# Routing steps inside an attention loop: a table laid out the other way round, built a unit later, and VectorE's routing steps put after its attention steps

## The chip, the cores and the metric

One core of a Trainium2 chip. The metric is the device time of one execution in microseconds, the median of several runs.

## The reference

A gated linear attention over 768 steps (4 batches, 8 heads of 40) gives 3072 rows of 320 numbers. Each row goes through a mixture of 8 experts (two of them for each row, chosen by noisy logits), each expert being a product 320 to 1024, a ReLU and a product 1024 to 320:

```python
C = f_stab * C + i_stab * einsum('bhd,bhe->bhde', v_t, k_t);  n = f_stab * n + i_stab * k_t
y_t = sigmoid(o_t) * (C @ q_t) / maximum(abs(n . q_t), 1)          # 768 steps, 32 (batch, head) pairs
logits = x @ w_gate + log1p(exp(x @ w_noise)) * noise
top2, top2_w = the two largest logits and their softmax
out[mask_e] += top2_w * (relu(x[mask_e] @ w1[e]) @ w2[e])          # for each expert e
```

## The kernel before

**Attention, units 0 to 23.** The sequence is cut into 12 chunks of 64 steps; a unit is one chunk of 16 (batch, head) pairs, so there are 24 units. The loop `while i < NU - LEAD` runs 22 of them, the last two are written out after it. The order of every engine is the order in which the program is written; nothing is rescheduled. In unit i TensorE (PE) does `c_part` (L385, state update), `o_part` (L394, output of the unit), the first `e_part` product (L334, gate exponents of unit i+2), `l_part` (L437, gate logits), at times the ranks `r_part` (L446 to L448) or a burst `b_part` (L457), the transposes `t_part` (L417), the second `e_part` product, and `s_part` (L354, L357, scores of unit i+2). ScalarE (ACT) copies the state (`c_part`, L388), takes the exponentials (L337), part of the sigmoid (`sig_part`, L343), and copies the transposes (L421) and logits (L515). VectorE (DVE) does `k_part` (kd, L365), the three steps of `f_part` (dn, dn, tm: L399, L401, L405) and `p_part` (p, L371), which the next unit's `o_part` needs. GpSimd (POOL) multiplies by the gate (L406) and issues part of the DMAs. The second `e_part` product writes the same PSUM bank as the first, so it waits for the first exponential.

**Routing, between the attention's steps.** Every four units make a group with a generator `g_part(g)`: softplus of the noise (na, co, ln: L540 to L559), top two (MAX, MAX_INDEX: L567, L570), counts `m` and prefix sums `base`, a request for ranks, and from the ranks two one-hot tables in fp16: `OB` (128 places, L652) and `OA` (56 blocks of 128 places of the experts' lists, L646, times a signed token number, L649). The burst of the group is eight matmuls with `OB[:, :, j]` as weights and `OA[:, :, j]` as the moving operand; their sum is added to the table `TBL`, from which token lists are decoded and rows gathered. `fill(upto, much)` takes steps of the waiting generators up to a sum of assumed prices: 0.2 at the unit's start, 0.15 between the steps of `f_part`, and what is left of 1.6 at the unit's end. A generator that yields `"long"` goes on only at the unit's end; one that yields `"wait"` stops for this call. ScalarE's part of the routing (Exp, +1, Ln: three instructions at L712, and Exp of d) is held in a list `acts` and issued by `act`: what stood in it at the unit's start behind the unit's first exponential, the rest at the unit's end. `next(pre1)` in the units of `W1AT` splits a piece of the first expert's weights into a high part (ScalarE, L142, L144) and a low part (POOL, L145).

**Experts.** After the last unit expert 0 begins with the tokens of the first 12 units: eight products `mm1` (f = 0 to 7, each eight matmuls at L1022 into one of three PSUM banks; ScalarE L1033 and VectorE L1036 read it), then second-layer sums in three passes (L1138). In between, `advance` does the remaining groups' routing: ranks and bursts come due at a set distance (`lag`) after they are asked for. After the burst of group 4, VectorE adds to the table (L464) and decodes, POOL gathers the rows of two more tiles (L794), and TensorE transposes them (L824) in the third pass.

Of the kernel before, what the change touches and what calls it, by code (L numbers as in the profile page):

```python
# [9 lines left out]
BF = mybir.dt.bfloat16  # L10
HF = mybir.dt.float16
# [3 lines left out]
OP = mybir.AluOpType  # L15
# [3 lines left out]
NE, F, DM = 8, 1024, 320  # L19
# [8 lines left out]
TC = BLK // 128  # L28
# [28 lines left out]
W1LD, W1AT, W2AT = (6, 9, 12, 15, 18), (11, 13, 17, 19, 20, 21), 21  # L57

C_ID, C_DIM, C_TRI, C_ONE, C_I8, C_TOK, C_N, C_SGN, C_VAC, C_COL, C_END = 0, 128, 192, 320, 448, 456, 480, 608, 656, 712, 768
# [6 lines left out]
def build(ctx, tc, qk, vk, og, fi, noise, wgn, w1, w2, cst, ce, out):  # L66
    nc = tc.nc
    V, A, P, T, SP = nc.vector, nc.scalar, nc.gpsimd, nc.tensor, nc.sync
# [10 lines left out]
    cs = keep.tile([128, C_END], F32, name="cs")  # L79
# [4 lines left out]
    cols = keep.tile([128, NE * TC, 8], HF, name="cols")  # L84
    sgn = keep.tile([128, 2 * NU], HF, name="sgn")
# [253 lines left out]
    def sig_part(u, ps_=(0, 1, 2)):  # L339

        g = SG[u % 4]
        for p in ps_:
            A.activation(g, g, (AF.Exp, AF.Ln, AF.Exp)[p], bias=float(p == 1), scale=(-1.0, 1.0, -1.0)[p])  # L343
# [64 lines left out]
    def keep_rows(u):  # L408
        (P if u < XV - 1 else SP).dma_start(XD[128 * u:128 * u + 128, 0:DM], XR[u])
# [119 lines left out]
    OAT = [rt.tile([128, NE * TC, 8], HF, name=f"oa{i}", bufs=1) for i in range(2)]  # L529

    def g_part(g):
# [14 lines left out]
        while acts:  # L546
            yield "wait"
        co = sm("co", [128, nb, NE])
# [33 lines left out]
        m = sm("m", [128, NE, nb + 1], BF)  # L582
        V.tensor_add(m[:, :, 1:].rearrange("p e u -> p u e"), oh4[:, :, 0], oh4[:, :, 1])
        if u0 == 0:

            V.tensor_scalar(m[:, :, 0], cs[:, C_I8:C_I8 + 8], 32.0, None, op0=OP.mult)
        else:
            V.tensor_copy(m[:, :, 0], acc[g - 1])
# [5 lines left out]
        asked = [m[:, :, 1:], base[:, :, 0:nb], base[:, :, nb], rk, False, unit[0] + lag[0]]  # L594
        want.append(asked)
        yield
        while acts:
            yield "wait"
        dd = sm("dd", [128, nb])
# [34 lines left out]
        n = 2 * nb  # L634
# [6 lines left out]
        while done[0] < u0 - 4:  # L641
            yield "wait"
# [3 lines left out]
        V.tensor_tensor(OA, cols, ah[:, None, :].to_broadcast([128, C, n]), op=OP.is_equal)  # L646
        yield 0.3
        yield "long"
        V.tensor_mul(OA, OA, sgn[:, None, 2 * u0:2 * u0 + n].to_broadcast([128, C, n]))  # L649
        yield 0.3  # L650
# [3 lines left out]
        bursts.append(([OB[:, :, j] for j in range(n)], [OA[:, :, j] for j in range(n)], unit[0] + lag[1]))  # L654
# [287 lines left out]
    sig_part(u + 1)  # L942
    keep_rows(u)
# [454 lines left out]
```

## Time and profile before

| what | us |
|---|---|
| median of 3 runs (517.52 to 518.98) | 517.7 |
| the profiled execution | 516.41 |
| its span, first to last instruction | 514.5 |
| TensorE busy in the span | 498.1 (97%) |
| VectorE, ScalarE, POOL busy | 332.2, 246.4, 231.2 |
| attention, as the units run | to about 127 |

The profile tells for each engine when each instruction ran and what it had waited for. A bracket such as `[0.42 <-DVE p L371]` behind a row is idle time of that engine just before it, and the instruction that ended it. Matmuls overlap and their ends are modelled, so a busy TensorE can hide short delays: the time from start to start tells more than the bracket. The granted clock is 0.997 of full speed over the span.

### The profile page before, as it was taken

Reading aid. Unit: us, or ns where it says so; the run is one execution under the profiler, and the core shown is the slowest. Engines: PE = TensorE matmul, PEld = TensorE weight load, DVE = VectorE, ACT = ScalarE, POOL = GpSimd, SP = SyncE. Lnnn points to the kernel's source line nnn. Section 1 sums busy time; section 2 is a strip of 40 time slices with the busy share of each in tenths; the row PEclk is TensorE's granted clock in tenths of the full one; section 3 lists DMA queues with packets and bytes.
Section 4 is the critical chain, followed back from the end, with each engine's and each line's share of the span. In section 5 each row is a group of like instructions: output and inputs, shape, how many; then the busy total and the mean of one; then the engine's idle time right before and its main releaser. Section 6 shows DMA issues by size and latency. Waiting matters only on the chain.

```text
span 514.5 us, 13117 instructions
## 1 busy us (share of the span) xinstructions
PE 498.1 (97%) x5042; PEld 471.6 (92%) x5043; DVE 332.2 (65%) x933; ACT 246.4 (48%) x568; POOL 231.2 (45%) x303
## 2 busy tenths in 40 slices
PE   8799999999999999999999999999999999999995
PEld 3588888888989998999999999999999999999994
DVE  7888889889695686754854584376538347555410
ACT  7689878889613354433541553153335405514300
POOL 9666674374034676156225604540562255142033
PEclk9999999999999999999999999999999999999998
DMA  6899787886848375196149406832951583282033
GB/s 168 234 277 250 220 240 192 231 229 204 314 134 261 70 96 184 46 245 145 41 99 270 104 16 160 209 89 52 268 101 49 129 234 89 56 177 26 2 35 47
DMA packets 51621, 77.06 MB, mean 150 GB/s; under 512 B 10825, under 2 KB 41936, under 8 KB 51520
## 3 DMA queue, kind: packets, MB, share of 16 engines
q1 hardware_dynamic: 38576, 50.16, 33.4%
q0 software_dynamic: 12976, 25.99, 24.8%
q8 instruction: 42, 0.69, 0.6%
q14 instruction: 27, 0.22, 0.1%
HBM read 52.27 MB, written 17.48 MB: 136 GB/s over the span
## 4 chain that ended last, share of the span: by engine, by line
PE 88%; DVE 3%; DMA 3%; POOL 2%; ACT 2%; issue 1%; SPq 0%; POOLq 0%; DVEq 0%
PE s L1022 25%; PE e L1022 12%; PE o L1054 5%; PE o L1053 5%; PE o L1052 5%; PE st L1054 5%; PE st L1052 5%; PE st L1053 5%; PE o L394 3%; PE s L357 3%; PE st L385 2%; PE e L334 2%; DMA vk<-vk_in 2%; PE xt L437 2%; PE xt L417 1%
## 5 line engine op out<-in xcount | busy, mean ns | idle before, releaser
L1075 POOL DMA_INDIRECT y_out<-y,tok x53 | 87.3, 1648 | 181.3 <-DVE y L1065 180.4
L1033 ACT ACTIVATE hx<-s 128x384 fp32r<-128x384 f32 (+5 forms) x91 | 44.4, 488 | 104.0 <-PE s L1022 66.7
L1022 PE MATMUL s<-xh,w1h 128*128 128x384 f32 (+5 forms) x273 | 76.4, 337 | 0.0
L1036 DVE SCALAR_TENSOR_TENSOR hx<-s,hx 128x384 fp32r<-128x384 f32 (+3 forms) x91 | 48.2, 529 | 36.5 <-ACT hx L1033 36.0
L794 POOL DMA_INDIRECT xg<-rows,tok x53 | 56.2, 1061 | 27.7 <-issue 12.8
L1022 PE MATMUL s<-xh,w1l 128*128 128x384 f32 (+5 forms) x273 | 62.4, 336 | 0.0
L1054 PE MATMUL o<-w2h,hx 128*128 128x320 f32 x184 | 56.8, 309 | 0.0
L1052 PE MATMUL o<-w2h,hx 128*128 128x320 f32 x184 | 56.8, 309 | 0.0
L1053 PE MATMUL o<-w2l,hx 128*128 128x320 f32 x184 | 56.7, 308 | 0.0
L1052 PE MATMUL st<-w2h,hx 128*128 128x320 f32 x176 | 54.4, 309 | 0.0
L1054 PE MATMUL st<-w2h,hx 128*128 128x320 f32 x176 | 54.4, 309 | 0.0
L1053 PE MATMUL st<-w2l,hx 128*128 128x320 f32 x176 | 54.2, 308 | 0.0
L1022 PEld LDWEIGHTS s<-xh,w1h 128*128 128x128 f32 x273 | 48.8, 188 | 1.8 <-ACT xh L826 0.3
L1022 PEld LDWEIGHTS s<-xh,w1l 128*128 128x128 f32 x273 | 47.8, 188 | 1.7 <-DVE xh L828 0.2
L1033 ACT ACTIVATE hx<-e 128x384 fp32r<-128x384 f32 (+5 forms) x45 | 22.1, 491 | 53.9 <-PE e L1022 36.7
L1022 PE MATMUL s<-xl,w1h 128*128 128x384 f32 (+5 forms) x182 | 46.3, 336 | 0.0
L1065 DVE TENSOR_SCALAR y<-o,gw 128x320 f32<-128x320 f32 x23 | 12.7, 551 | 47.2 <-PE o L1054 47.2
L1065 DVE TENSOR_SCALAR y<-st,gw 128x320 f32<-128x320 f32 x22 | 12.1, 551 | 43.5 <-PE st L1054 43.4
L1022 PE MATMUL e<-xh,w1h 128*128 128x384 f32 (+5 forms) x135 | 38.7, 341 | 0.0
L343 ACT ACTIVATE vk<-vk 128x320 f32<-128x320 f32 x72 | 33.8, 470 | 3.6 <-DMA vk<-og_in 2.7
L406 POOL TENSOR_TENSOR xr<-tm,vk 128x320 f32<-128x320 f32 x24 | 21.0, 875 | 30.9 <-ACT w L337 13.0
L1036 DVE SCALAR_TENSOR_TENSOR hx<-e,hx 128x384 fp32r<-128x384 f32 (+3 forms) x45 | 24.0, 534 | 16.4 <-ACT hx L1033 16.2
(243 smaller groups left out, 1252.4 us busy)
## 6 DMA issues: line engine op xcount, KB each, us to landing
raw<-w_in SPq DMA_DIRECT2D x6, 1280.0 KB
qk<-qk_in SPq DMA_DIRECT2D x24, 256.0 KB, 4.8
raw<-w_in SPq DMA_DIRECT2D x6, 1024.0 KB, 8.8
y_out<-zrow SPq DMA_DIRECT2D x15, 320.0 KB, 4.1
raw<-w_in SPq DMA_DIRECT2D x17, 256.0 KB, 9.7
vk<-vk_in POOLq DMA_DIRECT2D x24, 162.0 KB, 4.2
vk<-vk_in SPq DMA_DIRECT2D x24, 162.0 KB, 4.6
vk<-og_in SPq DMA_DIRECT2D x24, 160.0 KB, 4.2
```

The costliest lines, as they stand in the source:

```text
L343: A.activation(g, g, (AF.Exp, AF.Ln, AF.Exp)[p], bias=float(p == 1), scale=(-1.0, 1.0, -1.0)[p])
L357: T.matmul(SQ[u][:, p][half[p], h, :], q[r, 1, h, :], q[r, 0, h, :], start=True, stop=True)
L406: P.tensor_mul(XR[u], tm.rearrange("p h d -> p (h d)"), SG[u % 4])
L794: P.indirect_dma_start(out=XG[0:rows_of(t), t], out_offset=None, in_=XD[0:n], in_offset=bass.IndirectOffsetOnAxis(ap=token(e, t), axis=0), ...
L1022: T.matmul(ps[:, 0:n], l, r, start=i == 0, stop=i == len(ops) - 1)
L1033: A.activation(hi, x, AF.Relu)
L1036: V.scalar_tensor_tensor(lo, top[0], 0.0, top[1].bitcast(F32), op0=OP.max, op1=OP.subtract)
L1052: T.matmul(ps, HH[:, j, c], W2H[:, j], start=j == 0, stop=False)
L1053: T.matmul(ps, HH[:, j, c], W2L[:, j], start=False, stop=False)
L1054: T.matmul(ps, HLO[:, j, c], W2H[:, j], start=False, stop=j == 7)
L1065: V.tensor_scalar(y[0:n], ps[0:n], GW[e][0:n, t:t + 1], None, op0=OP.mult)
L1075: st = P.indirect_dma_start(out=out, out_offset=bass.IndirectOffsetOnAxis(ap=token(e, t), axis=0), in_=y[0:n], in_offset=None, compute_op= ...
```

## The change

- `OA` is now laid out `[128, 8, 56]`, so that each matmul's moving operand is 56 numbers in a row; before it was every eighth number of `[128, 56, 8]`. The one-hot comparison goes into a new tile `ohc` in the old layout, and the multiplication by the token number reads `ohc` with its last two axes turned.
- Both table steps and `OB` wait for the next unit (`unit[0] == begin`).
- Two new `"long"` marks, behind the waits for ScalarE: the steps from `co` on, and those from `dd` on, now go only at a unit's end, after `p`.
- The first column of `m` is written by POOL, ahead of `co`, and no longer by VectorE after the one-hots.
- Group 4's ranks (asked for in unit 19) come one unit later. `W1AT` becomes 11, 12, 16, 19, 20; the sixth piece is done in the written-out unit 22.

```diff
-W1LD, W1AT, W2AT = (6, 9, 12, 15, 18), (11, 13, 17, 19, 20, 21), 21
+W1LD, W1AT, W2AT = (6, 9, 12, 15, 18), (11, 12, 16, 19, 20), 21
-    OAT = [rt.tile([128, NE * TC, 8], HF, name=f"oa{i}", bufs=1) for i in range(2)]
+    OAT = [rt.tile([128, 8, NE * TC], HF, name=f"oa{i}", bufs=1) for i in range(2)]
...
         while acts:
             yield "wait"
+        yield "long"
+        m = sm("m", [128, NE, nb + 1], BF)
+        if u0 == 0:
+            P.tensor_scalar(m[:, :, 0], cs[:, C_I8:C_I8 + 8], 32.0, None, op0=OP.mult)
+        else:
+            P.tensor_copy(m[:, :, 0], acc[g - 1])
         co = sm("co", [128, nb, NE])
...
-            V.tensor_copy(m[:, :, 0], acc[g - 1])
...
-        asked = [..., rk, False, unit[0] + lag[0]]
+        asked = [..., rk, False, unit[0] + lag[0] + (unit[0] == 19)]
...
         while acts:
             yield "wait"
+        yield "long"
         dd = sm("dd", [128, nb])
...
-        while done[0] < u0 - 4:
+        begin = unit[0]
+        yield
+        while done[0] < u0 - 4 or unit[0] == begin:
             yield "wait"
...
-        V.tensor_tensor(OA, cols, ah[:, None, :].to_broadcast([128, C, n]), op=OP.is_equal)
+        OH = sm("ohc", [128, C, n], HF)
+        V.tensor_tensor(OH, cols, ah[:, None, :].to_broadcast([128, C, n]), op=OP.is_equal)
...
-        V.tensor_mul(OA, OA, sgn[:, None, 2 * u0:2 * u0 + n].to_broadcast([128, C, n]))
-        yield 0.3
+        V.tensor_mul(OA, OH.rearrange("p c j -> p j c"), sgn[:, 2 * u0:2 * u0 + n, None].to_broadcast([128, n, C]))
+        yield 0.5
...
-        bursts.append(([OB[:, :, j] for j in range(n)], [OA[:, :, j] for j in range(n)], unit[0] + lag[1]))
+        bursts.append(([OB[:, :, j] for j in range(n)], [OA[:, j] for j in range(n)], unit[0] + lag[1]))
...
     sig_part(u + 1)
+    next(pre1)
     keep_rows(u)
```

VectorE in unit 10 (dn, dn, tm, p are the attention's; co to nl and the MAX are group 1's routing; kd is the next unit's), before and after:

```order
L399 RECIPROCAL dn<-o 128x8
L549 SCALAR_TENSOR_TENSOR co_1379<-t_4_1320,ue_1319 128x32
L401 SCALAR_TENSOR_TENSOR dn<-dn 128x8
L551 RECIPROCAL na_1317<-t_4_1320 128x32
L405 SCALAR_TENSOR_TENSOR tm<-dn,o 128x320
L371 TENSOR_TENSOR p<-s,w 128x1024
L553 TENSOR_TENSOR co_1379<-co_1379,na_1317 128x32
```

```order
L399 RECIPROCAL dn<-o 128x8
L401 SCALAR_TENSOR_TENSOR dn<-dn 128x8
L405 SCALAR_TENSOR_TENSOR tm<-dn,o 128x320
L371 TENSOR_TENSOR p<-s,w 128x1024
L556 SCALAR_TENSOR_TENSOR co_1431<-t_4_1331,ue_1330 128x32
L558 RECIPROCAL na_1318<-t_4_1331 128x32
L560 TENSOR_TENSOR co_1431<-co_1431,na_1318 128x32
```

co and na, which need ScalarE's three routing instructions, moved from between dn and tm to behind p. ScalarE in unit 14 and at the start of unit 15 (w is an exponential, ue, t and ln are group 2's routing, share copies a burst's result, vk the state and the sigmoid), before and after:

```order
L337 ACTIVATE w<-e 128x512
L712 ACTIVATE ue_1743<-na_1741 128x32
L712 ACTIVATE t_4_1744<-ue_1743 128x32
L712 ACTIVATE ln_1745<-t_4_1744 128x32
L421 ACTIVATE xts<-xt 128x384
L515 ACTIVATE lg<-xt 128x16
L466 ACTIVATE share<-xt 128x56
L337 ACTIVATE w<-e 128x512
L343 ACTIVATE vk_114<-vk_114 128x320 x2
L388 ACTIVATE vk_111<-st 40x328 x2
```

```order
L337 ACTIVATE w<-e 128x512
L421 ACTIVATE xts<-xt 128x384
L515 ACTIVATE lg<-xt 128x16
L466 ACTIVATE share<-xt 128x56
L337 ACTIVATE w<-e 128x512
L717 ACTIVATE ue_1758<-na_1745 128x32
L717 ACTIVATE t_4_1759<-ue_1758 128x32
L717 ACTIVATE ln_1760<-t_4_1759 128x32
L343 ACTIVATE vk_114<-vk_114 128x320 x2
L388 ACTIVATE vk_111<-st 40x328 x2
```

The three moved from behind the unit's first exponential to behind its second, ahead of the next unit's state copy. VectorE in expert 0 around the last first-layer product, f = 7 (hx from bank e; rank to ob are group 4's, ln and nl group 5's), before and after:

```order
L632 TENSOR_SCALAR ai_2983<-rank 128x8
L1036 SCALAR_TENSOR_TENSOR hx<-s_2961,hx 128x384
L1114 TENSOR_TENSOR w2l<-raw_122,w2h 128x320
L637 SCALAR_TENSOR_TENSOR bi_2998<-ai_2983,rank 128x8
L640 CAST ah_3000<-ai_2983 128x8
L646 TENSOR_TENSOR oa_218<-cols,ah_3000 128x448
L649 TENSOR_TENSOR oa_218<-oa_218,sgn 128x448
L652 TENSOR_TENSOR ob_216<-spot,bi_2998 128x1024
L1036 SCALAR_TENSOR_TENSOR hx<-e,hx 128x384
L1114 TENSOR_TENSOR w2l<-raw_122,w2h 128x320
L559 TENSOR_TENSOR ln_2934<-ln_2934,nzt 128x32
```

```order
L634 TENSOR_SCALAR ai_2994<-rank 128x8
L1042 SCALAR_TENSOR_TENSOR hx<-e,hx 128x384
L1120 TENSOR_TENSOR w2l<-raw_122,w2h 128x320
L639 SCALAR_TENSOR_TENSOR bi_3003<-ai_2994,rank 128x8
L642 CAST ah_3005<-ai_2994 128x8
L651 TENSOR_TENSOR ohc_3009<-cols,ah_3005 128x448
L654 TENSOR_TENSOR oa_218<-ohc_3009,sgn 128x448
L657 TENSOR_TENSOR ob_216<-spot,bi_3003 128x1024
L556 SCALAR_TENSOR_TENSOR co_3021<-t_4_2964,ue_2963 128x32
L558 RECIPROCAL na_2942<-t_4_2964 128x32
```

The read of bank e for f = 7 now stands ahead of the table steps; group 5's steps from co on stand behind them. On TensorE the ranks of group 4 moved from behind f = 6 to behind f = 7, and its burst from the first pass of the sums to the second.

## Rows read from the trace of the kernel before

**Rows 1.** Busy time in the units' stretch: us, each engine's busy (instructions), clock.

```profile
26.00:123.30 97.30, 94.34 (x2244) 84.08 (x2240) 84.99 (x264) 83.08 (x216) 57.01 (x92) 1.00 0.87 233
```

**Rows 2.** Timeline of PE: start, us, instruction, count, [idle before <- what ended it].

```profile
74.88 0.18 PE L447 MATMUL xt<-base,ones 128*128 128x32 bf16 x1 [0.23 <-DVE base L591]
...
76.70 0.84 PE L385 MATMUL st<-vk,kd 104*40 104x41 f32 x32
77.96 1.13 PE L394 MATMUL o<-vk,p 104*64 104x41 f32 x32 [0.42 <-DVE p L371]
...
82.79 1.13 PE L394 MATMUL o<-vk,p 104*64 104x41 f32 x32 [0.22 <-DVE p L371]
...
87.37 0.81 PE L385 MATMUL st<-vk,kd 104*40 104x41 f32 x31
88.01 0.22 PE L394 MATMUL o<-vk,p 128*64 128x41 f32 x1
...
113.98 0.18 PE L446 MATMUL xt<-m,tri 128*128 128x32 bf16 x1 [0.41 <-DVE m L588]
...
120.16 0.50 PE L334 MATMUL e<-re,le 98*128 98x512 f32 x1 [0.48 <-ACT w L337]
```

**Rows 3.** The bursts and the ranks by line: duration ns min/median/max, first and last start.

```profile
L457 PEld LDWEIGHTS <-ob x48: 142/147/208, 65.0 to 158.9; 128*128 128x128 f16 x48
L447 PEld LDWEIGHTS <-ones x6: 95/95/101, 55.9 to 149.1; 128*128 128x128 bf16 x6
```

**Rows 4.** Timeline of the weight loads, the first burst.

```profile
65.03 0.90 PEld L457 LDWEIGHTS <-ob 128*128 128x128 f16 x8
```

**Rows 5.** Busy time of L712 in unit 14: us, ScalarE busy (instructions).

```profile
84.00:86.00 2.00, 0.69 (x3) 1.00 0.59 173
```

**Rows 6.** Timeline of ScalarE, units 10, 14 to 15, and 21.

```profile
67.09 0.62 ACT L337 ACTIVATE w<-e 128x512 f32<-128x512 f32 x1
...
87.19 0.99 ACT L343 ACTIVATE vk<-vk 128x320 f32<-128x320 f32 x2
88.25 0.89 ACT L388 ACTIVATE vk<-st 40x328 f32<-40x328 f32 x2
...
122.17 0.63 ACT L142 ACTIVATE w1h<-raw 64x512 fp32r<-64x512 f32 x1
```

**Rows 7.** Timeline of VectorE, units 10 and 11.

```profile
65.76 0.19 DVE L549 SCALAR_TENSOR_TENSOR co<-t,ue 128x32 f32<-128x32 f32 x1 [1.22 <-ACT t L712]
...
67.68 0.29 DVE L553 TENSOR_TENSOR co<-co,na 128x32 f32<-128x32 f32 x1
...
71.04 1.40 DVE L375 TENSOR_TENSOR p<-s,w 64x512 f32<-64x512 f32 x2
```

**Rows 8.** Timeline of POOL, a weight split in units 11 to 12.

```profile
72.92 1.27 POOL L145 TENSOR_TENSOR w1l<-raw,w1h 128x512 fp32r<-128x512 f32 x1 [0.80 <-DMA qk<-qk_in]
```

**Rows 9.** Timeline of VectorE in the same stretch, and the next kd.

```profile
73.04 1.26 DVE L583 TENSOR_TENSOR m<-oh 128x32 bf16<-128x32 f32 x1
...
74.75 0.80 DVE L365 TENSOR_TENSOR kd<-vk,w 128x640 f32<-128x640 f32 x1
```

**Rows 10.** The multiplication by the token number, by line: duration ns min/median/max.

```profile
L649 DVE TENSOR_TENSOR oa<-oa,sgn x6: 391/392/394, 59.8 to 152.9; 128x448 f16<-128x448 f16 x6
```

**Rows 11.** Timeline of PE in expert 0, the sums' first and third pass.

```profile
145.66 0.85 PE L1138 MATMUL e<-w2h,hx 128*128 128x320 f32 x4 [1.09 <-DVE hx L1036]
...
153.78 0.49 PE L824 MATMUL s<-cs,xg 128*128 128x128 f32 x3
```

**Rows 12.** The chain that ended last, one first-layer product (start, us, instructions).

```profile
136.28 1.40 PE e L1022 x8
```

**Rows 13.** Timeline of VectorE, table and decoding for the fifth group.

```profile
148.40 0.18 DVE L464 TENSOR_TENSOR tbl<-tbl,o 128x56 f32<-128x56 f32 x1
```

**Rows 14.** Timeline of POOL, the first of two gathers.

```profile
149.74 1.10 POOL L794 DMA_INDIRECT xg<-rows,tok  x1 [0.87 <-DVE km L488]
```

**Rows 15.** All gathers by line: time from issue to landing.

```profile
DMA to landing us min/median/max: 2.0/3.1/6.9
```

More of the change, by code (lines that the diff above doesn't have):

```diff
@@ L580, in g_part @@
             yield "wait"
-        m = sm("m", [128, NE, nb + 1], BF)
         V.tensor_add(m[:, :, 1:].rearrange("p e u -> p u e"), oh4[:, :, 0], oh4[:, :, 1])
-        if u0 == 0:
-            V.tensor_scalar(m[:, :, 0], cs[:, C_I8:C_I8 + 8], 32.0, None, op0=OP.mult)
-        else:
-            V.tensor_copy(m[:, :, 0], acc[g - 1])
         yield
@@ L593, in g_part @@
         rk = sm("rk", [128, NE * nb + 8])
-        asked = [m[:, :, 1:], base[:, :, 0:nb], base[:, :, nb], rk, False, unit[0] + lag[0]]
+        asked = [m[:, :, 1:], base[:, :, 0:nb], base[:, :, nb], rk, False, unit[0] + lag[0] + (unit[0] == 19)]
         want.append(asked)
```

## The prediction

> **What bounds the kernel now.** I read the busy time by stretch first. In the units' stretch TensorE is busy 94.34 of 97.30 us and the clock is full [rows 1]: TensorE is the bound, and what an engine beside it saves counts only where TensorE waits. All its idle time there is 97.30 − 94.34 = 2.96 us, the ceiling for what the rearrangement can win in the attention. The timeline of TensorE says where some of it lies and who ends it [rows 2]: ranks waiting for `base` 0.23, o_part of unit 13 waiting for p 0.42, o_part of unit 14 0.22, ranks waiting for m 0.41, a second e product waiting for its exponential 0.48. All but the last end with VectorE. The brackets are low: from state product to o_part takes 77.96 − 76.70 = 1.26 us where there is a wait, 88.01 − 87.37 = 0.64 where there is none, so 0.62 lost under a bracket of 0.42, a factor of 1.48. Third, the bursts: a weight load from `ob` takes 147 ns where one from `ones` takes 95 [rows 3], and eight take 0.90 us [rows 4], a pitch of (0.90 − 0.147) / 7 = 0.108. Last, expert 0: TensorE waits 1.09 us for VectorE's read of bank e [rows 11]. In the sum below, + is time saved.
>
> **Bursts.** Two things are strided at 16 bytes now: the moving `OA[:, :, j]` and the weights `OB[:, :, j]`. Only OA becomes contiguous. If the moving side holds the pair, the pitch falls at most by what a strided weight load has over a plain one: 0.147 − 0.095 = 0.052 [rows 3], to an estimated 0.056, so 8 × 0.052 = 0.41 a burst. Of six bursts (48 loads) three stand in the attention, one (group 4's) is followed by a wait of TensorE in the new order, two more stand where TensorE is the bound: 5 × 0.41 = **+2.05**; bounds 0 (the weight side holds it) and 2.2. I take the upper part because a load already lasts longer than the pitch, 147 against 108 ns [rows 3, 4]: loads overlap, so their duration need not set it. No row decides it.
>
> [...]
>
> **VectorE's steps at the end of a unit.** In unit 10 co waits 1.22 us for ScalarE [rows 7] with the attention's steps queued behind it; in the new order they go first. With the wait for `base` (first m column now on POOL), the p wait, the m wait and the e wait (the weight piece that stood before it is moved) that is 0.23 + 0.42 + 0.41 + 0.48 = 1.54 by brackets, × 1.48 = **+2.28**. Bounds: 0.8 (half, the rest taken over by something a little later) and 2.3.
>
> **ScalarE's triple.** Exp, +1 and Ln take 0.69 us together [rows 5]. They stood behind a unit's first exponential, where ScalarE next waits for the transposes; now they stand in front of the sigmoid, the next unit's state copy and its first exponential. There ScalarE has little to give: the sigmoid ends at 87.19 + 0.99 = 88.18, the state copy starts at 88.25 [rows 6], a gap of 0.07. The second e product of the next unit waits for that exponential, as it does at 120.16 [rows 2]. So each of units 7, 11, 15 and 19 may lose between 0 and 0.69. Unit 11 has the longest gap on ScalarE and I count it free; for the three others I take 0.3, less than half, because ScalarE's gaps are 97.30 − 84.99 = 12.31 us of the stretch [rows 1], 0.56 a unit over 22 units, and some of the 0.69 goes into them: 3 × 0.3 = **−0.9** (0 to −2.1).
>
> **co and what follows it.** The triple now starts behind the second exponential and three instructions at their old pitch of about 0.25 put the answer t near 67.09 + 0.98 = 68.07, where co started at 65.76 [rows 6, 7]. co and na, 0.49 by the pair, then come before L553, which starts at about 68.56 instead of 67.68: 0.88 later. The timeline shows no idle time of VectorE from there to p for unit 12 at 71.04, which lasts 1.40 to 72.44 [rows 7] and whose o_part was due at about that time. Unit 12's o_part is 0.88 late. In the same place of the later groups p has some room; I take 0.4 for the two together: **−1.28** (0 to −2).
>
> **Weight pieces.** In unit 12 POOL now runs a low part (1.27 us [rows 8]) while VectorE does rank steps. What this does to VectorE the trace shows: a step of 128x32 took 1.26, from 73.04 to 74.30, and ended when POOL's piece did, 72.92 + 1.27 = 74.19 [rows 8, 9]. Then kd follows (0.80) and p. Unit 12 got room at its end, since the two table steps (391 ns each, the second's row [rows 10]; the first is of the same shape) go to unit 13: 1.26 − 0.78 = 0.48 late, **−0.48**. Bounds: nothing is held and unit 14's 0.22 wait goes as well (+0.33), or only one table step's room counts (−0.87). In unit 22 the sixth piece's two copies (0.63 each, [rows 6]) stand in front of the copy of the transposes, whose answer the logits product needs: between 0 and −1.26, I take **−0.5**, since ScalarE waits for TensorE before that copy anyway.
>
> **Table steps themselves.** The product now reads `ohc` with its axes turned. Its price is between 0.39, as now (448 numbers [rows 10]), and 0.61: kd's 640 numbers took 0.80 [rows 9]; were that one number per x and the present product two per x, both with a fixed part f, then 640x + f = 0.80 and 224x + f = 0.392, x = 0.98 ns, f = 0.172, and 448x + f = 0.61. I take 0.61; the 0.22 go into a unit's end three times, hidden by the step that left it, and once into expert 0's chain, inside the bounds there.
>
> [...]
>
> **Expert 0.** VectorE's read of bank e for f = 7 no longer stands behind three table steps: the wait at 145.66 goes, **+1.09** [rows 11]. But group 4's ranks come one product later, 1.40 [rows 12], and its burst in the second pass, so the addition to the table (148.40 [rows 13]) and the gathers (149.74 [rows 14]) come 1.40 later while TensorE comes 1.09 earlier. A gather lands 3.1 us after its issue in the median [rows 15]: before, 152.84, 0.94 ahead of the transposes at 153.78 [rows 11]. Now the transposes wait 1.40 + 1.09 − 0.94 = 1.55: **−1.55**. With 2.0 to landing it is 0.45, with 6.9 it is 5.35 [rows 15]. Net −0.46: the gain turns into a new wait eight microseconds later.
>
> **Sum.** 2.05 + 2.28 − 0.9 − 1.28 − 0.48 − 0.5 + 1.09 − 1.55 = +0.71. Against the profiled execution of 516.41 (span 514.5 and 1.9 around it) that is 515.7; the median of the runs, 517.7, lies 1.3 above that execution, and the same saving from it gives **517.0**.
>
> **Rivals.**
> - A, clearly faster: the triple fits into ScalarE's gaps (+0.9), POOL's piece holds nothing on the path (+0.4 of the 0.48), and TensorE's own delays give co half its lateness back (+0.64): 517.0 − 1.94 = 515.1. For it: 12.31 us of gaps on ScalarE and 13 on VectorE [rows 1]. Against it: the 0.07 gap of [rows 6] just where the triple goes.
> - B: the weight loads keep the pitch at 0.108 and the first term is nothing: 517.0 + 2.05 = 519.1, a little slower than before. It decides if the eight loads of a burst still take 0.90. For it: 147 ns is longer than the pitch [rows 3, 4]; against it: the matmul of the pair reads at the same stride, so the rows do not tell which of the two holds it.
> - C, clearly slower: group 4's gather lands as the slowest did, 6.9 us after issue instead of 3.1 [rows 15]. TensorE cannot reorder past the transposes, so it waits 3.8 longer: 520.8. From about 5.4 to landing on, the kernel is slower by over 0.3%. Before, 0.94 of room hid part of that; now none does.
> - D, the change doesn't do what it says: VectorE's waits only move, p being late by other steps behind the second exponential, and the second term is nothing: 517.0 + 2.28 = 519.3. For it: the same step co, later, on an engine with no gap in [rows 7].
>
> **How the numbers follow.** Forecast 0.46, A 0.30, B 0.10, C 0.05, D 0.09. About 0.3%, 1.55 us, is what a measurement of this kernel can tell from no change: below 516.15 is faster, above 519.25 slower. Faster: A, 0.30. Slower: C, and half each of B and D, which lie at the line: 0.05 + 0.05 + 0.05 = 0.15. The same: the rest, 0.55. The range reaches from A to D, 515.0 to 519.3; it leaves out C, some of A's lower side and half of D, about 0.2.
>
> **What the profile after will show.** Eight loads of a burst in about 0.54 us (0.147 + 7 × 0.056), or 0.90 if B. No idle of VectorE before co of the 1.2 us kind, and no idle of TensorE before o_part of unit 13 nor before m's ranks; but some before o_part of unit 12 with p as its end, and before the second e product in units 7, 15, 19 with the exponential as its end. A VectorE step of over 1 us under L145 in unit 12. In expert 0 no wait before L1138's first sums, and a wait of about 1.5 us before L824. The product with `ohc` at 0.6 us. The prediction is wrong if the bursts' pitch does not fall, if ScalarE's triple costs TensorE nothing or its whole 0.69 four times, or if the wait before L824 is absent or above 2.5.

## The result: slower by 0.7%, outside the range, and the profile after

The median of 21 runs of the changed kernel is 524.43 us, beside 520.51 us of 21 runs of the kernel before on the same chip: ratio 1.0074 (95% interval 1.0054 to 1.0094). The prediction was 517.0 (515.0 to 519.3), the likeliest case "the same". The sign and the range are both missed.

The profiled execution took 523.28 us (span 521.5) where that of before took 516.41 (514.5), 7.0 us of span more. That is more than the medians differ by (3.92): 516.41 lies below every one of the 21 runs of before (517.45 to 522.55). The busy time of the changed kernel by stretch (us, busy of PE, PEld, DVE, ACT, POOL with instructions, granted clock, DMA share, GB/s): the units; expert 0's first-layer products of the first tile; its second-layer sums; the second tile's products; the second layer of that tile; the third tile; the rest.

```profile
26.00:123.30 97.30, 92.15 (x2175) 81.55 (x2173) 86.29 (x253) 81.06 (x214) 57.62 (x95) 1.00 0.85 233
129.00:143.43 14.43, 14.17 (x93) 13.18 (x92) 10.63 (x47) 9.24 (x29) 2.55 (x4) 1.00 0.73 256
143.43:158.58 15.15, 13.95 (x94) 11.86 (x93) 10.67 (x54) 3.26 (x10) 5.28 (x8) 1.00 0.50 150
158.58:167.35 8.77, 8.69 (x74) 8.26 (x73) 7.44 (x29) 3.31 (x10) 0.00 (x0) 1.00 0.89 299
167.35:176.05 8.70, 8.46 (x57) 7.93 (x58) 3.13 (x18) 1.19 (x3) 6.12 (x6) 1.00 0.30 80
176.05:196.25 20.20, 17.16 (x122) 16.56 (x122) 12.97 (x47) 7.31 (x19) 13.66 (x16) 0.92 0.45 69
196.25:521.50 325.25, 319.01 (x1970) 312.40 (x1968) 178.62 (x422) 116.80 (x248) 125.37 (x138) 0.99 0.48 115
```

The first row answers to [rows 1]: TensorE is busy 92.15 instead of 94.34 us, with 2175 instead of 2244 of its instructions in the stretch. Before, the stretches from expert 0 on took 14.02, 14.04, 8.86, 8.25, 15.01 and 326.46 us, and the first product started at 127.86 instead of 129.00. So the 7.00 us of span are: to expert 0 +1.14, first products +0.41, sums +1.11, second tile −0.09, its second layer +0.45, **third tile +5.19**, the rest −1.21.

The third tile is read from TensorE first (start, us, instruction, idle before and what ended it), with the last group's burst ahead of it:

```profile
165.58 0.68 PE L457 MATMUL o<-oa,ob 128*128 128x56 f16 x8
...
173.57 0.40 PE L829 MATMUL xt<-cs,xg 64*128 64x64 f32 x3
...
174.88 0.49 PE L829 MATMUL s<-cs,xg 128*128 128x128 f32 x3
...
178.93 0.56 PE L829 MATMUL xt<-cs,xg 128*128 128x128 f32 x3
182.52 0.44 PE L1028 MATMUL e<-xh,w1h 128*128 128x192 f32 x2 [3.04 <-DVE hx L1044]
```

TensorE stands still 3.04 us for VectorE's read of a bank, and that stands behind ScalarE's. ScalarE in the same stretch (L831 copies transposes of gathered rows, L1039 reads a product):

```profile
172.80 0.49 ACT L831 ACTIVATE xh<-s 128x384 fp32r<-128x384 f32 x1 [5.08 <-PE s L829]
175.67 0.33 ACT L831 ACTIVATE xh<-xt 128x192 fp32r<-128x192 f32 x1 [2.38 <-PE s L829]
179.94 0.49 ACT L831 ACTIVATE xh<-s 128x384 fp32r<-128x384 f32 x1 [3.94 <-PE xt L829]
180.33 0.33 ACT L1039 ACTIVATE hx<-e 128x192 fp32r<-128x192 f32 x1
```

The transposes that the second of these copies needs ended at 173.97, those for the third at 175.37 (173.57 + 0.40 and 174.88 + 0.49 on TensorE). The answers come 1.70 and 4.57 us later. What the brackets name is only the last event before the start, no operand. GpSimd meanwhile issues seven gathers in a row, then a scatter; before, the first of them started at 160.69, beside the second tile's products:

```profile
168.38 1.07 POOL L799 DMA_INDIRECT xg<-rows,tok  x1 [9.99 <-DVE over L678]
...
176.33 1.01 POOL L799 DMA_INDIRECT xg<-rows,tok  x1 [0.30 <-issue]
...
177.64 1.63 POOL L1081 DMA_INDIRECT y_out<-y,tok  x1 [0.19 <-issue]
```

And the idle time costs a second time, as the granted clock (the figure behind POOL) falls after it. The same view, finer:

```profile
179.50:182.50 3.00, 0.00 (x0) 0.01 (x1) 1.96 (x8) 1.54 (x5) 0.00 (x0) 1.00 0.47 55
182.50:183.50 1.00, 0.98 (x9) 1.00 (x9) 1.00 (x5) 0.00 (x0) 0.85 (x1) 0.99 0.00 0
183.50:184.00 0.50, 0.50 (x5) 0.50 (x4) 0.50 (x5) 0.30 (x1) 0.34 (x1) 0.50 0.00 0
184.00:186.00 2.00, 2.00 (x11) 2.00 (x11) 1.39 (x7) 0.36 (x2) 1.67 (x3) 0.50 0.37 102
```

The granted clock is 0.50 from 183.50 to past 186, after TensorE had done nothing for 3 us; up to 182.50 it was 1.00. The third tile's 20.20 us hold 20.20 − 17.16 = 3.04 us of idle time and 17.16 − 15.01 = 2.15 us of longer work: together the 5.19. Not all of the 2.15 is the clock. The three products behind the wait, in the changed kernel and then in the kernel before (whose row also counts three transposes that are still running):

```profile
182.52:186.87 4.35, 4.35 (x24) 4.35 (x25) 3.39 (x15) 0.66 (x2) 3.73 (x5) 0.61 0.18 50
```

```profile
175.93:178.67 2.74, 2.74 (x27) 2.74 (x26) 2.42 (x13) 1.44 (x4) 2.24 (x4) 1.00 0.25 69
```

So the lower clock costs 4.35 − 2.74 = 1.61 us. The other 0.54 lies ahead of the wait, at full clock.

### The profile page after: what moved, and what is told of

Same layout as the page of the kernel before. It is cut to its first block, busy times and chain, and to the rows that moved or that the text cites. A ratio compares the mean times of both kernels' runs of the same rounds, so it can differ in the third digit from the quotient of the medians.

```text
span 521.5 us, 13116 instructions
## 1 busy us (share of the span) xinstructions
PE 499.7 (96%) x5042; PEld 470.3 (90%) x5043; DVE 336.1 (64%) x927; ACT 245.1 (47%) x568; POOL 232.3 (45%) x309
## 3 DMA queue, kind: packets, MB, share of 16 engines
q1 hardware_dynamic: 38576, 50.16, 32.6%
q0 software_dynamic: 12976, 25.99, 23.9%
## 4 chain that ended last, share of the span: by engine, by line
PE 81%; ACT 6%; DVE 5%; POOL 3%; issue 2%; DMA 1%; SPq 0%; POOLq 0%; DVEq 0%
PE s L1028 24%; PE e L1028 12%; PE o L1060 5%; PE o L1059 5%; PE o L1058 5%; PE st L1060 5%; PE st L1059 5%; PE st L1058 5%; PE o L394 3%; PE s L357 2%; PE st L385 2%; PE e L334 2%; ACT vk L343 2%; PE xt L437 1%; ACT w L337 1%
## 5 line engine op out<-in xcount | busy, mean ns | idle before, releaser
L1039 ACT ACTIVATE hx<-s 128x384 fp32r<-128x384 f32 (+5 forms) x91 | 44.3, 488 | 104.0 <-PE s L1028 63.4
L1028 PE MATMUL s<-xh,w1h 128*128 128x384 f32 (+5 forms) x273 | 77.6, 341 | 0.0
L1039 ACT ACTIVATE hx<-e 128x384 fp32r<-128x384 f32 (+5 forms) x45 | 22.1, 490 | 53.0 <-PE e L1028 32.4
L1058 PEld LDWEIGHTS o<-w2h,hx 128*128 128x128 f32 x184 | 34.6, 188 | 0.2 <-issue 0.2
```

What stands on the lines that cost most here:

```text
L1028: T.matmul(ps[:, 0:n], l, r, start=i == 0, stop=i == len(ops) - 1)
L1039: A.activation(hi, x, AF.Relu)
L1058: T.matmul(ps, HH[:, j, c], W2H[:, j], start=j == 0, stop=False)
```

## Experiments

Theory L: the loss is the **late last burst**. One term of the change lets the ranks asked for in unit 19 come a unit later. (They are group 3's; the part on the change calls them group 4's.) With it, and with the tables' wait of a unit, the last group's burst goes from behind the second product of expert 0's second tile to behind the seventh, and the seven gathers behind it go from 160.69 to 168.38. Rival W: the waits in the attention and in expert 0's first tile, which the prediction priced, are dearer than it said. Rival O: the new layout of OA costs more on VectorE than it gives TensorE.

**The term taken back (two runs of the same kernel).**

```diff
-        asked = [..., rk, False, unit[0] + lag[0] + (unit[0] == 19)]
+        asked = [..., rk, False, unit[0] + lag[0]]
```

> The changed kernel with one term taken back: group 3's ranks in unit 20 again instead of 21. By the order of TensorE this alone brings the last group's burst back from behind the seventh product of the second tile to behind the second. Theory L (the loss of the changed kernel is the last burst: expert 1's gathers were issued at 168.4 instead of 160.7, TensorE waited 3.04 us at 182.5 and ran at half clock for 3 us after it): gathers near 160.5, no wait of over 0.5 us between 175 and 200, full clock there, ratio to before 0.995 to 1.001. Rival U (the loss lies in the attention's units, where the changed kernel was 1.5 us behind at unit 21): the wait at 182 goes but the kernel stays slower, ratio 1.003 or more.

> The changed kernel with group 3's ranks in unit 20, so that the last burst stands behind the second product again, once more beside the changed kernel. Theory L: no stop, ratio 0.998 to 1.002, 4 to 5 us below the changed kernel where that has the stop. Rival N: the same ratio as the changed kernel.

Measured 0.9997 (0.9978 to 1.0016) and 0.9977 (0.9948 to 1.0006). The last burst is back behind the second product. Its gathers start at 165.66 and 165.28, 4.74 and 4.85 us behind the start of the second tile's products, as before (160.69 − 155.92 = 4.77; the changed kernel has 9.80). The third tile takes 15.03 and 15.02. Nothing else of the change was taken away, so W and O as main causes fall: what is left of the change costs nothing that can be told. The term holds a part of W too, as expert 0's first tile is about 1 us shorter without it (28.55 and 28.44 us instead of 29.58).

**The late burst alone, on the kernel before (two runs).**

```diff
-        bursts.append((..., unit[0] + lag[1]))
+        bursts.append((..., unit[0] + lag[1] + 10 * (u0 + nb == NU)))
```

> The kernel before with one number: the last group's burst comes due 10 steps later, behind the seventh product of the second tile, as in the changed kernel; nothing in the attention is touched. Theory L: a wait of about 3 us for expert 1's transposes near 180 and a clock under full behind it, 4 to 6 us more in the profile, ratio 1.006 to 1.011. Rival U: the transposes find their rows in time, ratio within 0.998 to 1.002.

> The kernel before with the last group's burst ten steps later, once more, beside the changed kernel. In three of four profiles of the changed kernel ScalarE and VectorE answered TensorE 1.5 to 3 us late between 172 and 182, in the stretch in which GpSimd issues the nine last gathers, TensorE then waited 2.1 to 3.0 and ran at half clock for 3 us. Theory L (the late last burst brings this about, on chips where it occurs): if the changed kernel shows the stop here, this one shows it too, 4 to 5 us, ratio 1.006 or more; if the changed kernel does not, neither does this. Rival N (it has nothing to do with the burst): the changed kernel has it and this one has not.

Measured 0.9997 (0.9972 to 1.0022), then 1.0076 (1.0042 to 1.0110). The first run spoke against L: the burst stood behind the seventh product and nothing happened. In the second, TensorE and ScalarE look like the changed kernel's:

```profile
179.89 0.44 PE L1022 MATMUL e<-xh,w1h 128*128 128x192 f32 x2 [2.41 <-DVE hx L1038]
```

```profile
173.72 0.33 ACT L826 ACTIVATE xh<-xt 128x192 fp32r<-128x192 f32 x1 [2.05 <-PE xt L824]
177.31 0.49 ACT L826 ACTIVATE xh<-s 128x384 fp32r<-128x384 f32 x1 [3.26 <-issue]
```

The burst stands at 163.96, behind the seventh product, and the third tile takes 19.54 us. The late burst alone therefore brings the whole loss, but not at all times.

**The changed kernel again (four runs, no edit).**

> The changed kernel once more, beside the three others on the same chip. Theory L: the wait for expert 1's gathers of about 3 us and the lower clock behind it stand in this profile too, ratio 1.005 to 1.010. Rival U or chance: the wait at 182 was of one execution alone, and the stops of 1.7 us without a releaser in unit 19 come again.

> The changed kernel a third time. Its first profile had ScalarE idle for 3.9 us at 176 to 180 with its operand there, and TensorE's clock low behind it; its second had not. Theory S (this stop is not the program's but comes in some executions): no stop or a stop elsewhere, ratio 1.000 to 1.003 where it is rare and 1.006 or more where it is common. Theory L (late gathers): ruled out if the stop is gone with the gathers as late as before.

> The changed kernel as the control of the other three: with the stop behind the last gathers a ratio of 1.006 to 1.010, without it 1.000 to 1.003.

> The changed kernel once more, as the yardstick for the two runs beside it. Both theories: seven gathers in a row on GpSimd from about 168, a scatter behind them 10.9 us after the first one's start, ratio to before about 1.007 where late answers of ScalarE occur (in nine profiles so far the last late answer starts 10.8 to 11.9 us after the first of the seven gathers); 1.001 where they don't.

Measured 1.0013 (0.9993 to 1.0034), 1.0101 (1.0080 to 1.0121), 1.0072 (1.0033 to 1.0111) and 0.9996 (0.9965 to 1.0026). The runs were made in four series, each on one chip: the first held the first run of the term taken back, of the late burst and of the changed kernel; the second and third those with 1.0101, 1.0076 and 1.0072; the fourth the last. The first and the third carry the same chip number in the record, so the chip alone does not tell them apart. The profile with 1.0101 is of the shortest of its seven runs (520.24). In the first and fourth series the changed kernel costs nothing. Its profile from the first series has the gathers at the same place, and ScalarE's two copies on time:

```profile
169.24 1.07 POOL L799 DMA_INDIRECT xg<-rows,tok  x1 [9.96 <-DVE over L678]
```

```profile
174.83 0.33 ACT L831 ACTIVATE xh<-xt 128x192 fp32r<-128x192 f32 x1 [0.71 <-PE xt L829]
176.23 0.49 ACT L831 ACTIVATE xh<-s 128x384 fp32r<-128x384 f32 x1 [1.07 <-PE s L829]
```

Late answers are in nine profiles: the changed kernel's with the result and all eight of the second and third series. There the last late answer of ScalarE starts 10.8 to 12.2 us after the first of the seven gathers, whether the gathers start at 162.68 or at 173.21. They are in none of the other nine, where the same copies start 0.03 to 0.04 us behind the transposes that they need. Only both together, late answers and a late burst, make the loss. Expert 0's second layer of the second tile and its third tile take together (us; all profiles but those of the three kernels with two gathers issued later, below):

| | last burst behind the seventh product | behind the second |
|---|---|---|
| late answers | 27.2 to 29.6 (five profiles) | 24.2 to 24.7 (four) |
| none | 23.2 to 23.3 (three) | 23.2 to 23.3 (three) |

So late answers take about 1 us from a kernel with an early burst as well. In line with that, the kernel before takes 520.51 us beside the result, 520.67 and 520.73 in the second and third series, and 519.10 and 519.23 in the other two. Its one profile is from none of the first three, so this is not shown.

One more thing divides the profiles in the same way. The nine without late answers record a time from issue to landing for most or some kinds of DMA (7 to 30 lines of the DMA view), the nine with them for no DMA at all, whatever its queue. One kind of load that has nothing to do with the gathers, in the first series' profile of the changed kernel and in that with the result (the last number of the first line is the time to landing):

```profile
qk<-qk_in SPq DMA_DIRECT2D x24, 256.0 KB, 5.7
```

```profile
qk<-qk_in SPq DMA_DIRECT2D x24, 256.0 KB
```

The packets that the two dynamic queues moved are the same in all 18 (12976 and 38576). So it is not the gathers alone: what the profile has of the ends of DMAs differs between the series. Whether that delays ScalarE, or the recording itself does, or all come from another thing, no run settles.

**Why an early burst is harmless even then.** The second run of the term taken back was made in the third series, beside 1.0072 and 1.0076. Its late answers (ScalarE, then the one wait of TensorE that follows from them):

```profile
172.53 0.38 ACT L1039 ACTIVATE hx<-s 128x256 fp32r<-128x256 f32 x1 [2.47 <-remote]
177.09 0.49 ACT L831 ACTIVATE xh<-s 128x384 fp32r<-128x384 f32 x1 [4.18 <-remote]
```

```profile
172.96 0.41 PE L1058 MATMUL o<-w2h,hx 128*128 128x320 f32 x1 [0.48 <-ACT hx L1039]
```

They are as late as the others, but lie beside second-layer products, of which TensorE has 24 to a tile without an answer to wait for: it waits 0.48 us there and 0.41 at the transposes, and the second layer takes 9.64 us instead of about 8.2. With the late burst they lie at the third tile, where every product fills one of three banks and the fourth waits for ScalarE and VectorE.

**The layout of OA alone, on the kernel before.**

```diff
-    OAT = [rt.tile([128, NE * TC, 8], HF, ...) for i in range(2)]
+    OAT = [rt.tile([128, 8, NE * TC], HF, ...) for i in range(2)]
...
-        V.tensor_tensor(OA, cols, ah..., op=OP.is_equal)
+        OH = sm("ohc", [128, C, n], HF)
+        V.tensor_tensor(OH, cols, ah..., op=OP.is_equal)
-        V.tensor_mul(OA, OA, sgn[:, None, ...])
+        V.tensor_mul(OA, OH.rearrange("p c j -> p j c"), sgn[:, ..., None])
```

> The kernel before with the layout alone: OA contiguous for each matmul, the comparison in a table of its own and the turned multiplication; every step stays in its place. Term 1 of the prediction: eight loads of a burst in about 0.54 us instead of 0.90, 5 to 6 bursts, 2.0 to 2.2 us less, ratio 0.996. The turned multiplication 0.61 us instead of 0.39. Rival (the weight side holds the pair): 0.90, ratio 1.000.

Measured 1.0004 (0.9984 to 1.0025). Eight loads take 0.64 us, so the bursts gain as in the changed kernel; the multiplication takes 0.969 in the mean, and in expert 0 the wait before bank e's sums, 1.09 in [rows 11], becomes

```profile
151.17 0.85 PE L1139 MATMUL e<-w2h,hx 128*128 128x320 f32 x4 [1.63 <-DVE hx L1037]
```

Expert 0's first tile takes 29.46 us instead of 28.06; the bursts, and the experts after the first (325.27 instead of 326.46 us, see the unread table below), give that back. Rival O is real in its parts and nothing in sum.

**Tables that don't wait a unit, and no later ranks.**

```diff
-        while done[0] < u0 - 4 or unit[0] == begin:
+        while done[0] < u0 - 4:
...
-        asked = [..., rk, False, unit[0] + lag[0] + (unit[0] == 19)]
+        asked = [..., rk, False, unit[0] + lag[0]]
```

> The changed kernel without both delays: group 3's ranks in unit 20 and the tables in the unit in which their ranks come. ScalarE's triple is then behind the unit's first exponential again. Theory T (the triple's place costs 0.37 us in each of units 15 and 19 and 0.46 in unit 12): from state product to state product these units take 4.40, 4.40 and 5.16 again, while the gains of units 13 and 18 (0.4 each) may stay; ratio 0.996 to 0.999. Rival: the 0.37 belong to VectorE's late co, and stay.

Measured 1.0036 (1.0007 to 1.0065), the second series: above the expected 0.996 to 0.999, and why is open. ScalarE's triple is back behind a unit's first exponential. From state product to state product, unit 15 to 16 takes 4.41 instead of 4.77 us, so the triple costs 0.36 where it stands now; 12 to 13 takes 4.62 instead of 5.62. The single profile is of no use for the sum, because TensorE stops several times for nothing that the trace shows, the largest of them:

```profile
117.84 0.32 PE L394 MATMUL o<-vk,p 128*64 128x41 f32 x5 [2.00 <-issue]
```

**The price of the turned reading.** Six operations on 448 fp16 numbers each were added to the last expert of the changed kernel, twice over, with results that nothing uses; one run.

```diff
+   V.tensor_mul(OA, OH turned, factor at step 0)         # as in the change
+   V.tensor_mul(OA flat, OH flat, cols flat)
+   V.tensor_mul(OA, OH flat, factor at step 0)
+   V.tensor_mul(OA, OH turned, cols flat)
+   V.tensor_mul(OA turned, OH flat, factor at step 1)
+   V.tensor_copy(OA, OH turned)
```

> The changed kernel with six operations of VectorE on 448 fp16 numbers added in the last expert (f = 1 to 6 of both halves), each writing OA, for durations alone: the turned multiplication as it is (0.97 expected), a multiplication of flat operands (0.39), flat operand times the broadcast factor with step 0 innermost, turned operand times a flat one, the old form with a turned write, a turned copy. If the read at step 8 is what costs, the first and the fourth take about 0.97 and the third 0.39 to 0.6; if the broadcast factor costs, the third takes 0.97 and the fourth less.

VectorE's timeline, in the order of the six, except that the first stands last (its second time):

```profile
480.54 0.38 DVE L1218 TENSOR_TENSOR oa<-ohc,cols 128x448 f16<-128x448 f16 x1
481.71 0.62 DVE L1220 TENSOR_TENSOR oa<-ohc,sgn 128x448 f16<-128x448 f16 x1
483.11 0.96 DVE L1222 TENSOR_TENSOR oa<-ohc,cols 128x448 f16<-128x448 f16 x1
484.84 2.24 DVE L1224 TENSOR_TENSOR oa<-ohc,sgn 128x448 f16<-128x448 f16 x1
487.76 0.56 DVE L1226 COPY oa<-ohc 128x448 f16<-128x448 f16 x1
490.44 0.95 DVE L1216 TENSOR_TENSOR oa<-ohc,sgn 128x448 f16<-128x448 f16 x1
```

Flat 0.38; a factor at step 0 makes it 0.62; reading at step 8 (16 bytes) makes it 0.95 to 0.96 whatever the factor, while a plain copy that reads so takes 0.56. The turned write goes through the new OA at a step of 56 numbers (112 bytes) and costs 2.24; a write at step 8 was not tried. The 0.61 that was estimated is close to the 0.62 of the flat reading with a factor at step 0; the 0.96 − 0.62 = 0.34 that the turned reading adds was left out.

**An unread table beside the kernel before (two runs).** The rest of the experts ran 1.2 us shorter in the profiles with the layout of OA, whose only trace there is the 896 bytes a partition of `ohc`.

```diff
+        sp = sm("ohc", [128, C, n], HF)
+        if g == 0:
+            P.memset(sp, 0.0)
```

> The kernel before with one table more in SBUF (128x448 fp16, written once by GpSimd, never read), so that everything allocated behind it lies where it lies in the changed kernel; the order is untouched. In four profiles the experts after the first ran 284.0 us between the same two outputs where ohc exists and 285.3 where it does not, with the same instructions. Theory P (place in SBUF): the experts take 1.2 to 1.4 us less here too. Rival (the chip or the execution of the day): 285.3 as in the kernel before.

> The kernel before with the unread table of 896 bytes a partition, once more. Theory P: the experts 1.3 us less again, and a ratio of 0.994 to 0.998. Rival: the gain of the last time was the chip's, 1.000.

Measured 0.9944 (0.9920 to 0.9968) and 0.9955 (0.9922 to 0.9989): faster than both kernels, both times in a series with late answers. A second-layer matmul, of before and then of this kernel (line, form, count, busy us, mean ns of one, idle before):

```profile
L1052 PE MATMUL st<-w2h,hx 128*128 128x320 f32 x176 | 54.4, 309 | 0.0
```

```profile
L1055 PE MATMUL st<-w2h,hx 128*128 128x320 f32 x176 | 53.6, 305 | 0.0
```

With the table one of three matmuls of a second layer is 4 ns shorter: 360 × 4 = 1.4 us, against the 1.2 that the rest gains. That it is the place in SBUF of what lies behind the table was the theory; no run shows a buffer's place. Besides the table the edit holds one memset on GpSimd, in the attention. In the four profiles without the table the experts after the first take 326.5 to 326.9 us, in the fourteen with it 325.2 to 325.9. The ratio's 2.3 to 2.9 us are more than that, and what lies over 1.2 has no row.

**Two of the seven gathers issued later (three kernels).**

```diff
-    gather(1, ts=tiles(0, 1))
     y = [mm2(0, 3)]
...
+        if f == 3:
+            gather(1, ts=tiles(0, 1))
```

> The changed kernel, with two of the seven gathers (expert 1's fourth and fifth tile) issued four products later, so that only five stand in a row and the scatter follows 2 x 1.31 = 2.6 us earlier. If ScalarE's late answers belong to the row of gathers, the last late one starts about 8.2 to 9.3 us after the first gather instead of 10.8 to 11.9, the second wait of TensorE at the third tile shrinks from 2 to 3 us towards nothing, and the time is 2 to 5 us below the changed kernel's beside it. If they belong to the stage (to the third tile's products, whatever GpSimd does), the wait and the time stay within 1 us of the changed kernel's.

> The kernel before with its last burst ten steps later, as in the earlier run, and the same two gathers issued four products later. If the row of gathers is the cause: 2 to 5 us less than the 1.0076 that the late burst alone cost, so 0.998 to 1.004. If it is the stage: 1.0076 again.

> The kernel before with the unread table of 896 bytes a partition and the two gathers issued four products later: a candidate for a version that beats both. The table alone gave 0.9944 and 0.9955; its late answers lay beside second-layer products and cost TensorE at most 0.4 to 0.7 us. If shorter rows of gathers make fewer late answers: 0.993 to 0.996. If they don't matter with an early burst: 0.994 to 0.996, not to be told apart from the table alone.

Measured 1.0204 (1.0159 to 1.0249), 1.0230 (1.0183 to 1.0276) and 1.0189 (1.0117 to 1.0261). The edit defeats the test: on GpSimd's queue the two gathers, the sixth and seventh of the row, now stand behind four more scatters. They start at 190.00 and 191.36, where the changed kernel of the same series has them at 174.98 and 176.29, and TensorE waits for their rows, in the first of the three:

```profile
190.00 1.06 POOL L799 DMA_INDIRECT xg<-rows,tok  x1 [0.30 <-issue]
```

```profile
193.37 0.87 PE L829 MATMUL xt<-cs,xg 128*128 128x128 f32 x3 [7.47 <-DMA xg<-rows,tok]
```

And the series was one without late answers, as the changed kernel's 0.9996 in it shows, so that there was nothing to make smaller. Whether a shorter row of gathers would help stays open. What the three show by accident is the clock again: in the first, after 7.47 us of nothing, 0.57 over the next 3.6 us; in the other two, after 7.45 and 7.54, second-layer matmuls of 0.47 us instead of 0.31.

## Why the prediction was wrong

**The step that failed is "Expert 0".** It followed group 4's burst with its addition, decoding and gathers one product later, and took the last group's burst as a mere 0.41 gained "where TensorE is the bound". The order of the changed program moves this burst too, from behind the second product of the second tile to behind the seventh. Its seven gathers were not priced at all. Their rows were in time, indeed: the first transposes that need them run at 172.27, 3.9 us after the issue, and don't wait. But what runs beside the gathers changed from products that need no answer to products that do, and with ScalarE's late answers 5.19 us are lost there in the profile. Rival C had the right place and kind (expert 0, a gather, clearly slower) but the wrong group and mechanism, the landing and not ScalarE; it had 0.05. A second thing was missing from every term: after the wait of 3 us TensorE works at half clock, 1.61 of the 5.19. A range that let one wait of 3 us with its clock arise in expert 0 would have reached 517.0 + 5.2 = 522.2. That covers the difference, if not the number: beside the changed kernel the one before took 520.51, 2.8 more than the median that the prediction started from.

In the series without late answers the kernel measures 1.0013 and 0.9996, which is the forecast "the same". That is in part luck: expert 0's first tile loses 1.5 us that the text did not have, and the experts after the first gain 1.2, as they do with the unread table, which no term has. The remaining terms, by the changed kernel's own profile:

**Bursts: right direction, oversized.** The first burst's loads, and the turned multiplication by form:

```profile
64.92 0.64 PEld L457 LDWEIGHTS <-ob 128*128 128x128 f16 x8
```

```profile
L654 DVE TENSOR_TENSOR oa<-ohc,sgn 128x448 f16<-128x448 f16 x6 | 5.8, 971 | 0.2
```

0.64 against 0.90 [rows 4]: 0.26 a burst instead of 0.41. A load takes 168 ns now in the median, more than the 147 of [rows 3], while the pitch falls to (0.64 − 0.17) / 7 = 0.067. So the moving side held most of the pitch, and rival B falls; a load's duration did not set the pitch, as was argued. The multiplication took 0.97, not the estimated 0.61: no row of before has a turned reading.

**VectorE's steps at a unit's end: right in which waits go, not in what they are worth.** The waits for `base`, for unit 13's p and for m's ranks [rows 2] are in none of the changed kernel's profiles. VectorE still waits for ScalarE ahead of co, now behind p, so that nothing of the attention stands behind it:

```profile
67.64 0.19 DVE L556 SCALAR_TENSOR_TENSOR co<-t,ue 128x32 f32<-128x32 f32 x1 [1.28 <-ACT t L717]
```

"No idle before co of the 1.2 us kind" was thus wrong in its wording. New waits come at the predicted place, o_part of unit 12, and at unit 14, which the list of signs did not have; the e product at 121.66 waits as the one at 120.16 did [rows 2]:

```profile
72.21 0.28 PE L394 MATMUL o<-vk,p 64*64 64x41 f32 x2 [0.23 <-DVE p L375]
72.85 1.12 PE L394 MATMUL o<-vk,p 64*64 64x41 f32 x30 [0.36 <-DVE p L375]
...
82.89 1.13 PE L394 MATMUL o<-vk,p 104*64 104x41 f32 x32 [0.75 <-DVE p L371]
...
121.66 0.50 PE L334 MATMUL e<-re,le 98*128 98x512 f32 x1 [0.50 <-ACT w L337]
```

Unit 12 to 13 takes 5.62 instead of 5.16 us: 0.46 against the 0.88 of the text. Units 13 and 14 together give back 0.21 (10.46 instead of 10.67), unit 18 to 19, with a burst, 0.44. In two of the other four profiles of this kernel o_part of unit 21 waits too, 1.09 and 0.62 us, with `dd` as its end.

**Weight pieces: the first right, the second nothing.** VectorE's step of over 1 us stands beside POOL's piece as predicted:

```profile
78.07 1.28 POOL L145 TENSOR_TENSOR w1l<-raw,w1h 128x512 fp32r<-128x512 f32 x1
```

```profile
78.23 1.46 DVE L634 TENSOR_SCALAR ai<-rank 128x8 int32<-128x8 int32 x1
```

kd and p for unit 14 come behind it, and the wait at 82.89 is the result: 0.75 us here, 0.49 in three of the other four profiles of this kernel, against the 0.48 of the text. The sixth piece in unit 22, priced −0.5, costs nothing: from unit 22's state product to expert 0's first product it is 5.83 us in all five profiles, against 6.19 before.

**ScalarE's triple: right in two of three places.** 0.37 in unit 15 to 16 and 0.35 in 19 to 20, against 0.3 each. No bracket names it; it is seen from start to start, as the first exponential of unit 15 starts 2.63 instead of 2.25 us behind the state product, and the second e product 3.26 instead of 2.92. For unit 7 nothing can be told: it takes 4.4 to 5.2 us in profiles of either kernel. The text's 12.31 us of gaps on ScalarE are VectorE's, by the order of the columns in [rows 1]; ScalarE's are 97.30 − 83.08 = 14.22, or 0.65 and not 0.56 a unit.

**The attention's sum: not to be told from these profiles.** Of +0.35 predicted, −1.14 was measured. TensorE's stops that nothing in the trace ends are 2.02 us in this profile's units, the largest 1.03 at 114.77, and 0.48 in that of before; in other profiles of the same kernel they are 0.4 to 2.9. Without them it is −1.14 + 1.54 = +0.40, but that this lies near the forecast is chance: the start of expert 0 less these stops is 126.7 to 131.7 us in five profiles of the changed kernel, and 126.7 to 129.6 in four with the attention of before.

**Expert 0's first tile: the wait for bank e goes, other waits come.**

```profile
146.22 1.44 PE L1144 MATMUL e<-w2h,hx 128*128 128x320 f32 x8 [0.19 <-DVE hx L1042]
...
148.78 0.68 PE L457 MATMUL o<-oa,ob 128*128 128x56 f16 x8 [0.54 <-DVE ob L657]
...
156.19 0.55 PE L829 MATMUL s<-cs,xg 128*128 128x128 f32 x3 [0.31 <-DMA xg<-rows,tok]
```

0.19 instead of 1.09 [rows 11], as said. The transposes wait 0.31 and not 1.55. But the burst waits 0.54 for its table, whose multiplication takes 0.35 longer than priced, and weight loads of the third pass wait for low parts that VectorE makes behind the decoding (0.17 in TensorE's timeline). Products and sums together are 1.52 longer (29.58 against 28.06; 29.55 to 29.66 in all five profiles of this kernel), where the text had −0.41 − 1.09 + 1.55 = +0.05.

## What to carry to other kernels

When an order moves a transfer or its issue, ask not only whether its data come in time, but what then runs beside it: work that needs an answer every microsecond loses what work without answers hides, here a wait of 3.04 us against 0.48 and 0.41. A wait of some 3 us on TensorE is to be priced with the slower clock behind it, here 3.04 + 1.61. And when two series of runs of the same kernel give 1.000 and 1.007, compare only within a series, and repeat the deciding experiment in more than one.

## What the runs showed of the hardware that was not expected

- ScalarE answers TensorE 1.3 to 4.6 us late about the time that GpSimd issues seven indirect gathers, in nine profiles, and 0.03 to 0.04 in nine others of nearly the same programs; the nine with it record no landing of any DMA. The cause is open.
- With an unread table of 896 bytes a partition, one of three second-layer matmuls takes 305 instead of 309 ns, and the kernel that does nothing else is 0.9944 and 0.9955 of before. The cause is not shown.
- A multiplication that reads fp16 at a step of 16 bytes costs VectorE 0.96 against 0.38 us for 448 numbers; one that writes at a step of 112 bytes, 2.24.
- The granted clock was 0.50 from 183.50 to 186.80, after a wait of 3.04 us on TensorE (the profile with the result), and 1.00 from 187.20 on to 190; it was 0.66 over 3 us after a wait of 2.41 (the second run of the late burst), and 0.57 over 3.6 us after one of 7.47, then 1.00 over the next 4 (the changed kernel with two gathers issued later).
